# Gated attention and a token-mixing MLP on one core: fp32 loads of v and z with casts on ScalarE and GpSimd, and one more turned block of scores

## The chip, the cores and the metric

The kernel runs on one core of a Trainium2 chip. The metric is device time in microseconds (us) of one execution: the median of a few runs, with the profile of one execution beside it. Engines are named as in the profile: PE is TensorE (PEld its weight loads), DVE is VectorE, ACT is ScalarE, POOL is GpSimd, SP is SyncE, which here only issues DMAs.

## The reference

Inputs: u and v of 8 x 3200 x 256, z of 8 x 3200 x 64, and three weights, all fp32.

```
scores = (z @ z.T) / S                    # per batch, 3200 x 3200
attn   = relu(scores) ** 2
x      = u * (attn @ v)                   # 3200 x 256
W_tok  = einsum('bsd,btd->bst', x @ w_q, x @ w_k) / sqrt(64)
out    = relu(einsum('bst,btd->bsd', W_tok, x)) @ w_out
```

The second half has no nonlinearity between W_tok and x, so the kernel forms `(x @ w_k).T @ x` ("heads", 64 x 256) first and then multiplies `x @ w_q` by it.

## The kernel before, in words

**Tiles.** The 3200 rows of a batch are 25 row tiles of 128, in seven groups: six of 512 columns (4 row tiles) and one of 128. A tile of scores is one group's columns against one row tile. Two tiles make a pair. For a pair, `scores` (L258) puts two fp16 matmuls with 64 contraction rows side by side into a PSUM tile of two banks (two such tiles exist, shared with the later products); `first_stage` (L278) takes max(0, x) times a constant to `g` in SBUF, on ACT (L286) or DVE (L290); `second_stage` (L296) squares `g` to fp16 `at`, on ACT (L306) or POOL (L308). `at` has 16 buffers, `g` 7.

**Turned blocks.** Scores are symmetric, so the block of group gi against the rows of group gj is the transpose of the block the other way round. `is_turned` (L213) says which blocks are taken so: gj up to two groups beyond gi (`FAR`), or gj the last group; `SKIP` and `EXTRA` (L210) are exceptions. For such a block `at` is turned by DMA transposes on SP's queue (L330) into `tt` (seven homes; `ttl` for the last group), and when group gj comes, `second_product` (L345) takes its weights from there, without a score matmul of its own.

**Second product.** For each group and each of its two halves, 25 row tiles are multiplied with v and accumulated in PSUM (L351; four banks, two per half). `gate` (L361) copies the sums out (L368), adds the two halves of the contraction (L369) and multiplies by u on POOL (L388). Then x is turned by a DMA (L400), projected by w_q and w_k (L417), the keys turned (L436) and multiplied with x (heads, L455), and once a batch is done, mixed (L483), passed through relu (L505 to L511), projected by w_out (L521), scaled (L546 on DVE, L551 on ACT) and stored (L552).

**The order of the work.** All of it is written out by a planner that runs while the kernel is built. It keeps a clock for each engine (L586 to L592) and for SP's queue and the DMA engines (`move` and `send`, L616 to L627): a `move` has a time from which it may go, a due time, an issue time, a time on the DMA engines, what to do when it has landed (`LANDS` later), and a condition. `flush` sends the ripe move that is due first. `squares` (L695) and `choose` (L660) pick the engine of a square and of a first stage by the clocks. The main loop (L1029) takes, in turn, something of the later products, a pair, or a step of the second product; `lead` bounds how far pairs run ahead of the steps. The constants (`SPARE`, `BIAS`, `LATE`, `RING`, `UNTIL`, `XWAIT`) are weights of these choices, so altering one changes the order on every engine.

**v and z.** Batch 0 has its own loads (`load_first_z`, `load_first_v`). For batches 1 to 7, `batch_begun` (L843) has z loaded in one DMA (L156) and v in five of 5 row tiles (L150). These are issued by POOL and cast from fp32 to fp16 on the way. z is then turned by four DMA transposes on SP's queue (L163) to `zT`.

Of the kernel before, what the change touches and what calls it, by code (L numbers as in the profile page):

```python
# [10 lines left out]
FP32 = mybir.dt.float32  # L11
# [5 lines left out]
def kernel(  # L17
# [45 lines left out]
    pk = ctx.enter_context(tc.tile_pool(name="pk", bufs=3))  # L63
    pxt = ctx.enter_context(tc.tile_pool(name="pxt", bufs=NXT))
    pu = ctx.enter_context(tc.tile_pool(name="pu", bufs=2))
    pg = ctx.enter_context(tc.tile_pool(name="pg", bufs=7))
    psum = ctx.enter_context(tc.tile_pool(name="psum", bufs=3))
    pat = ctx.enter_context(tc.tile_pool(name="pat", bufs=NAT))
    ptt = ctx.enter_context(tc.tile_pool(name="ptt", bufs=1))
# [74 lines left out]
            nc.tensor.matmul(out=idle[:, 0:P], lhsT=blank, rhs=blank, start=True, stop=True)  # L144
        clock[PE] += 0.053 * cold() * n

    def load_v(b, n0, nn):
        if n0 == 0:
            vs[b] = pv.tile([P, NT, D], FP16, tag="v_sb", name="v_sb")
        nc.gpsimd.dma_start(out=vs[b][:, n0 : n0 + nn, :], in_=rows(v, b)[:, n0 : n0 + nn, :])  # L150

    ztimes = []
    ZTURNS = [(0, 0, 7), (1, 0, 7), (0, 7, 13), (1, 7, 13)]

    def load_z(b):
        nc.gpsimd.dma_start(out=zn[:, 1 : NT + 1, :], in_=rows(z, b))  # L156

    def turn_z(b, i):
        odd, m0, m1 = ZTURNS[i]
# [452 lines left out]

    def at_time(t, fn):
# [41 lines left out]

    FARDUE = 12.0
    SPLIT = 0.2
    UNTIL = 24.0

    def choose(a, d):  # L660
        t = shut() + LATE
# [33 lines left out]
    def squares():  # L695
        while pending and pending[0][0] <= clock[PE] + 0.3:
            ready, p, g = pending.pop(0)
            a, c = max(clock[ACT], ready), max(clock[POOL], ready)
            by_act = a + SPARE < c and (a + 1.06 <= shut() + LATE or a + 2.5 < c)
            ways = [by_act]  # L700
            if clock[PE] < UNTIL and max(a + 0.63, c + 1.05) + SPLIT < min(a + 1.06, c + 1.9):
                ways = [a < c, a >= c]
                done = max(give(ACT, ready, 0.63), give(POOL, ready, 1.05))
            else:
                done = give(ACT, ready, 1.06) if by_act else give(POOL, ready, 1.9)
            for (b, gi, gj, _, nn, _, _), turn in second_stage(p, g, ways):
# [3 lines left out]
                move(  # L710
                    done + SLACK, due + SLACK, 1.28, 0.21 * n, turn,
                    lambda t, x=(p, b, gi, gj, nn): block_landed(t, *x),
                    lambda x=(b, gi, gj): has_home(*x),
                )
            for x in tiles[2 * p : 2 * p + 2]:
                row_at[x] = done + 0.6
# [15 lines left out]
    def use_keys(b, gi):  # L732
        open_slot()
        ps = ps_tile("qk")
        prior = None
        if keyed and keys_at.get(keyed[0], 1e9) <= clock[PE]:
            prior = keyed.pop(0)
        projections(b, gi, ps, stop=not prior)
        clock[PE] += 0.44 if gi < LASTG else 0.24
        if prior:  # L740
            heads(*prior, ps, halves(gi))
            clock[PE] += 0.44 if prior[1] < LASTG else 0.11
        ready = clock[PE] + FROM_PE
        a, d = (max(clock[x], ready) for x in (ACT, DVE))
        by_act = a + 0.58 <= d + 0.69 or d + 0.69 > shut() + LATE + 0.6
        projections_out(b, gi, ps, by_act)
        done = give(ACT, ready, 0.58) if by_act else give(DVE, ready, 0.69)
        n = widths[gi] / P
        final = (b, gi) == (last, LASTG - 2)
        if not final:  # L750
            move(
                done + SLACK, done + 10.0, 1.28, 0.21 * n, lambda: turn_keys(b, gi),
                lambda t: at_time(t, lambda: double(b, gi)),
            )
            keyed.append((b, gi))
        if prior:
            heads_out(*prior, ps)
            done = give(DVE, done, 0.7)
            if prior[1] == LASTG:
                give(POOL, done, 0.6)  # L760
                heads_known(prior[0])
        close_slot(done)
        if len(keyed) == 2 and gi == LASTG:
            add_extra(done + 14.0, "heads", use_heads)
        if final:
            for _ in keyed[1:]:
                add_extra(done, "heads", use_heads)
# [49 lines left out]
    def project_out(b, gi, ps, ready):  # L817
# [11 lines left out]
            if gi < LASTG:  # L829
                stored[i] = t  # L830

        move(done + SLACK, done + 6.0, 0.55, 1.6, stores[0], landed)

    def push(takes):
        give(POOL, clock[PE], 0.6)
        dma_at[0] = max(dma_at[0], clock[PE]) + takes

    Z0 = 24
    ZWAIT, ZDUE, ZSTEP, ZSTEP0 = 14.0, 32.0, 7.0, 5.0
    V0 = 56  # L840
    V1 = 10

    def batch_begun(b, t):  # L843
        if b + 1 < B:
            t0 = max(t + 6, Z0)
            at_time(t0, lambda: (load_z(b + 1), push(3.0)))
            step = ZSTEP if b else ZSTEP0
            for i, (_, m0, m1) in enumerate(ZTURNS):
                move(
                    t0 + ZWAIT + step * i, t0 + ZDUE + step * i, 1.28, 0.21 * (m1 - m0),  # L850
                    lambda i=i: turn_z(b + 1, i),
                    lambda t, i=i: z_ready.update({(b + 1, i): t}),
                )
            for i in range(5):
                at = t + 20 + 13 * i if b else V0 + V1 * i
                at_time(at, lambda i=i: v_loaded(b + 1, 5 * i, 5))

    def v_loaded(b, n0, nn):
        load_v(b, n0, nn)
        push(2.5)  # L860
        for n in range(n0, n0 + nn):
            v_at[b, n] = dma_at[0] + 5.0

    z_ready = {}

# [4 lines left out]
    def group_begun(b, gi, t):  # L870
        if gi == 0:
            batch_begun(b, t)
        if gi + 1 < NG:
            move(max(t + 2, clock[POOL] + SLACK), t + 7, 0.55, 1.6, lambda: load_u(b, gi + 1))
        elif b + 1 < B:
            move(max(t + 2, clock[POOL] + SLACK), t + 7, 0.55, 1.6, lambda: load_u(b + 1, 0))

    SPARE = 0.5
    BIAS = 0.2
    XDUE = 5.0  # L880
    XWAIT = 2.0
    LATE = 0.5

    def half_done(b, gi, half):
        ready = clock[PE] + FROM_PE
# [9 lines left out]
        if half == halves(gi)[-1]:  # L895
            n = 8 if widths[gi] == W else 2
            move(
                t + SLACK, t + XDUE, 1.28, 0.21 * n, lambda: turn_x(b, gi),
                lambda t: x_landed(t, b, gi), lambda: len(xTs) < NXT,
            )  # L900

# [119 lines left out]
    move(10.0, 14.0, 0.55, 1.6, lambda: load_u(0, 0))  # L1021
# [153 lines left out]
```

## Time and profile before

| | |
|---|---|
| median of 3 runs | 774.47 us (774.18 to 778.38) |
| the profiled execution | 773.15 us |
| its span from first to last instruction | 770.9 us |
| mean granted TensorE clock in it | 0.997 |
| instructions | 28221 |
| bytes read from HBM, written to it | 59.64 MB, 26.21 MB |

The profile's page gives each engine's busy time and its share of the span, forty slices of the span in tenths, the DMA queues, the chain of waits that ended last, and the costliest groups of instructions by line with their mean duration in ns and the idle time of their engine before them. A busy TensorE is modelled: its matmuls are pipelined, so the chain is read beside it. Further views used below: busy time by stretch (length, then busy time and count of PE, PEld, DVE, ACT and POOL, granted clock, DMA share, GB/s), groups by line and shape, waits (who waited for whom: us in total, times, longest), one tile's instructions, and the chain in order of time (start, length, what).

### The profile page before, as it was taken

To read this page: it belongs to the slowest core of one execution; us is meant where nothing else is said; L and a number is where in the kernel's file an instruction comes from. 1 tells how busy PE (TensorE), PEld (TensorE's weight loads), DVE (VectorE), ACT (ScalarE), POOL (GpSimd) and SP (SyncE) were. 2 spreads that over 40 slices of the span, in tenths; PEclk is the share of its full clock that TensorE was granted. 3 is DMA by queue.
4 is the path that set the end of the run, shared out by engine and by line. 5 is a ranking of instruction groups with operands and counts; after the bars stand their busy time and mean duration, and the time that the engine had idled before them with its cause. 6 is when DMAs were issued, how large, how long until landed. Compare 5 with 4: busy or idle time off the path is not lost.

```text
span 770.9 us, 28221 instructions
## 1 busy us (share of the span) xinstructions
PE 761.7 (99%) x12408; PEld 678.4 (88%) x12408; DVE 510.5 (66%) x537; ACT 561.2 (73%) x647; POOL 591.1 (77%) x496
## 2 busy tenths in 40 slices
PE   8999999999999999999999999999999999999996
PEld 7889998888898888989889988998889989898884
DVE  6775876675787566765677756765667476675645
ACT  7785876778758678875788677877777676777734
POOL 8796788789687778666778687887878887888740
PEclk9999999999999999999999999999999999999998
DMA  8999999999999999999899999999999998979625
GB/s 199 130 187 182 167 204 173 160 212 194 194 162 189 194 209 190 182 213 203 153 190 162 188 231 163 219 145 160 262 156 192 184 190 211 201 143 203 152 84 191
DMA packets 307114, 141.09 MB, mean 183 GB/s; under 512 B 285744, under 2 KB 288432, under 8 KB 306992
## 3 DMA queue, kind: packets, MB, share of 16 engines
q1 hardware_dynamic: 300224, 123.13, 85.0%
q0 software_dynamic: 6624, 15.98, 14.8%
q8 instruction: 97, 1.59, 0.9%
q14 instruction: 25, 0.20, 0.1%
q10 hardware_dynamic: 144, 0.20, 0.1%
HBM read 59.64 MB, written 26.21 MB: 111 GB/s over the span
## 4 chain that ended last, share of the span: by engine, by line
PE 94%; POOL 2%; DVE 1%; DMA 1%; ACT 1%; issue 1%; POOLq 0%; SPq 0%; DVEq 0%; ACTq 0%
PE acc L351 68%; PE sc L263 13%; PE fo L521 6%; PE qk L417 3%; PE qk L455 2%; POOL at L308 2%; PE mx L483 1%; DMA z<-in_z_dram 1%; POOL x_sb L388 1%; DVE g L290 0%; ACT g L286 0%; DVE fo L546 0%; DMA xT_sb<-x_sb 0%; PE hd L455 0%; ACT at L306 0%
## 5 line engine op out<-in xcount | busy, mean ns | idle before, releaser
L351 PE MATMUL acc<-v_sb,at 64*128 64x256 f16 x7344 | 504.7, 269 | 0.0
L308 POOL TENSOR_TENSOR at<-g 128x1024 f16<-128x1024 f32 (+1 forms) x218 | 402.3, 1859 | 71.6 <-ACT g L286 29.1
L351 PEld LDWEIGHTS <-at 64*128 64x128 f16 x7344 | 407.2, 94 | 48.1 <-issue 4.8
L290 DVE TENSOR_SCALAR g<-sc 128x1024 f32<-128x1024 f32 (+2 forms) x285 | 338.5, 1203 | 122.8 <-PE sc L263 114.3
L306 ACT ACTIVATE at<-g 128x1024 f16<-128x1024 f32 (+2 forms) x255 | 257.2, 1023 | 21.8 <-DVE g L290 17.8
L286 ACT ACTIVATE g<-sc 128x1024 f32<-128x1024 f32 (+2 forms) x186 | 183.2, 989 | 76.8 <-PE sc L263 75.0
L388 POOL TENSOR_TENSOR x_sb<-both,u_sb 128x512 f16<-128x512 f32 (+1 forms) x112 | 135.8, 1217 | 81.6 <-DVE both L369 77.7
L263 PE MATMUL sc<-zT 64*128 64x512 f16 x924 | 188.1, 375 | 1.4 <-DVE g L290 0.6
L351 PE MATMUL acc<-v_sb,tt 64*128 64x256 f16 x2272 | 163.4, 269 | 0.0
L351 PEld LDWEIGHTS <-tt 64*128 64x128 f16 x2272 | 126.2, 94 | 10.3
L369 DVE TENSOR_TENSOR both<-acc,both 128x512 f32<-128x512 f32 (+1 forms) x104 | 69.6, 670 | 21.4 <-ACT both L368 17.0
L263 PEld LDWEIGHTS <-zT 64*128 64x128 f16 x924 | 61.2, 94 | 7.6 <-issue 3.9
L368 ACT COPY both<-acc 128x512 f32<-128x512 f32 (+1 forms) x69 | 39.0, 565 | 38.7 <-PE acc L351 36.1
L546 DVE TENSOR_SCALAR fo<-fo 128x1024 f32<-128x1024 f32 (+1 forms) x28 | 32.4, 1166 | 46.6 <-PE fo L521 46.6
L509 ACT ACTIVATE rt<-mx 128x1024 f16<-128x1024 f32 x39 | 39.9, 1024 | 12.6 <-PE mx L483 12.1
L521 PE MATMUL fo<-wo,rt 128*128 128x256 f16 x386 | 46.6, 273 | 0.5 <-ACT rt L505 0.5
L521 PEld LDWEIGHTS <-rt 128*128 128x128 f16 x386 | 36.2, 98 | 8.4 <-issue 3.6
L431 ACT CAST qk<-qk 128x512 f16<-128x512 f32 (+1 forms) x47 | 25.3, 539 | 24.6 <-PE qk L455 20.0
L368 DVE COPY both<-acc 128x512 f32<-128x512 f32 (+1 forms) x35 | 23.6, 674 | 21.2 <-PE acc L351 19.9
L470 DVE TENSOR_TENSOR ha<-qk,ha 128x512 f32<-128x512 f32 x37 | 25.5, 689 | 14.4 <-ACT qk L431 14.1
L551 ACT ACTIVATE fo<-fo 128x1024 f32<-128x1024 f32 (+2 forms) x23 | 22.5, 978 | 16.5 <-PE fo L521 15.8
L417 PE MATMUL qk<-xT_sb,wqk 64*128 64x256 f16 (+1 forms) x404 | 32.3, 265 | 0.0
(55 smaller groups left out, 282.9 us busy)
## 6 DMA issues: line engine op xcount, KB each, us to landing
u_sb<-in_u_dram SPq DMA_DIRECT2D x48, 512.0 KB, 4.8
out_dram<-fo SPq DMA_DIRECT2D x46, 512.0 KB, 5.1
v_sb<-in_v_dram POOLq DMA_DIRECT2D x35, 320.0 KB, 6.0
zn<-in_z_dram POOLq DMA_DIRECT2D x7, 400.0 KB, 7.8
tt<-at SPq DMA_TRANSPOSE x143, 4.7
u_sb<-in_u_dram SPq DMA_DIRECT2D x8, 128.0 KB, 2.9
out_dram<-fo SPq DMA_DIRECT2D x4, 256.0 KB, 3.3
xT_sb<-x_sb SPq DMA_TRANSPOSE x56, 5.4
```

What stands on the lines that cost most here:

```text
L263: nc.tensor.matmul(out=sc[h][:, 0:gw] if banks else sc[:, h, 0:gw], lhsT=z_cols(b, h, ti * P, P), rhs=z_cols(b, h, gs, gw), start=True, st ...
L286: nc.scalar.activation(out=g[:, hs, 0:w], in_=part, func=RELU, scale=GSCALE)
L290: nc.vector.tensor_scalar(out=g[:, hs, 0:w], in0=part, scalar1=0.0, scalar2=GSCALE, op0=AOP.max, op1=AOP.mult,)
L306: nc.scalar.square(out=out, in_=g[:, hs, 0:w])
L308: nc.gpsimd.tensor_mul(out=out, in0=g[:, hs, 0:w], in1=g[:, hs, 0:w])
L351: nc.tensor.matmul(out=accs[half, r][:, ds((j % 2) * D, D)], lhsT=weights(b, gi, ti, j)[top(r), :], rhs=vs[b][top(r), ti, :], start=(first ...
L368: copy(out=both[:, 0 : n * D], in_=accs[half, 0][:, 0 : n * D])
L369: nc.vector.tensor_add(out=both[:, 0 : n * D], in0=accs[half, 1][:, 0 : n * D], in1=both[:, 0 : n * D])
L388: nc.gpsimd.tensor_mul(out=xs[b, gi][:, 0:n, :, r, :].rearrange("p n c d -> p (n c) d"), in0=both[:, 0 : n * D].rearrange("p (m d) -> p m ...
L417: nc.tensor.matmul(out=ps[:, r, 0 : n * P], lhsT=wqk[top(r), c, :, :].rearrange("p t h -> p (t h)"), rhs=xTs[b, gi][top(r), 0:n, c, :], st ...
L509: nc.scalar.activation(out=out, in_=part, func=RELU)
L521: nc.tensor.matmul(out=banks[r][:, ds(j * D, D)], lhsT=flat[:, ds((dc * n + j) * P, P)], rhs=wo[:, dc, :], start=(dc == 0 and j == 0), sto ...
```

## The change

1. **Loads.** v and z of batches 1 to 7 are no longer cast in flight. They come as fp32 pieces on SP's queue into two staging tiles that alternate (3 and 2 row tiles of v, or 12 and 8 of z: 384 or 256 KB; the last piece of a z is 5 row tiles), one buffer each. When a piece has landed by the plan, ScalarE or GpSimd casts it to `v_sb` or `zn`. A piece is sent only when the plan has its staging tile free, and pieces go in a fixed order: per batch z in 3, then v in 10.
2. **One more turned block.** `EXTRA = [(0, 3)]`: in batches 1 to 7 the block of the first and the fourth group is turned too.
3. **Buffers.** `g` has 6 buffers in place of 7, and the staging tiles take 5 KB a partition.
4. **The planner's numbers.** A transpose of n blocks is planned as 0.2 + 0.13 n us of the DMA engines (0.21 n before); loads and stores 1.7 (1.6). `send` counts the DMA time from the end of the issue. `RING`, `SPARE`, `BIAS`, `XWAIT`, `LATE`, `UNTIL`, `lead` and the times of z's and v's loads are altered, and the third-issued load of v in batch 0 (row tiles 4 to 11) is planned at 6.2 instead of 9.0. `zn`'s border is cleared a second time, on GpSimd.

```diff
-    pg = ctx.enter_context(tc.tile_pool(name="pg", bufs=7))
+    pst = ctx.enter_context(tc.tile_pool(name="pst", bufs=1))
+    pg = ctx.enter_context(tc.tile_pool(name="pg", bufs=6))
...
-    def load_v(b, n0, nn):
-        if n0 == 0:
+    STAGES = (3, 2)
+    stage_of, parts = {}, []
+    turn = 0
+    for b in range(1, B):
+        for what, size in ((z, dqk), (v, D)):
+            n0 = 0
+            while n0 < NT:
+                nn = min(STAGES[turn] * D // size, NT - n0)
+                parts.append((b, what is v, n0, nn, turn))
+                n0, turn = n0 + nn, 1 - turn
+
+    def load_part(b, is_v, n0, nn, k):
+        if is_v and n0 == 0:
             vs[b] = pv.tile([P, NT, D], FP16, tag="v_sb", name="v_sb")
-        nc.gpsimd.dma_start(out=vs[b][:, n0 : n0 + nn, :], in_=rows(v, b)[:, n0 : n0 + nn, :])
+        stage = pst.tile([P, STAGES[k] * D], FP32, tag=f"st{k}", name="st")
+        size, what = (D, v) if is_v else (dqk, z)
+        stage_of[k] = stage[:, 0 : nn * size].rearrange("p (n d) -> p n d", d=size)
+        nc.sync.dma_start(out=stage_of[k], in_=rows(what, b)[:, n0 : n0 + nn, :])
+
+    def cast_part(b, is_v, n0, nn, k, by_act):
+        copy = nc.scalar.copy if by_act else nc.gpsimd.tensor_copy
+        out = vs[b][:, n0 : n0 + nn, :] if is_v else zn[:, 1 + n0 : 1 + n0 + nn, :]
+        copy(out=out, in_=stage_of[k])
...
-    EXTRA = []
+    EXTRA = [(0, 3)]
...
-    V3 = 9.0
+    V3 = 6.2
...
-    RING = 2.0
+    RING = 1.5
...
-        dma_at[0] = max(dma_at[0], begun) + takes
         sp_at[0] = max(begun + issue, dma_at[0] - RING)
+        dma_at[0] = max(dma_at[0], begun + max(issue, 0.9)) + takes
         if landed:
-            landed(max(sp_at[0], dma_at[0]) + LANDS)
+            landed(dma_at[0] + LANDS)
...
-    UNTIL = 24.0
+    UNTIL = 16.0
...
+            for i, x in enumerate(mine):
+                at = t0 + Z1 * i if not is_v else t + V2 + V3 * i if b else V0 + V1 * i
+                move(
+                    at, at + 8.0, 0.45, 0.2 + 1.5 * x[3] * (D if is_v else dqk) / 1024,
+                    lambda x=x: part_sent(*x),
+                    lambda t, x=x: at_time(t, lambda: part_landed(*x)),
+                    lambda x=x: parts[0] == x and stage_free[x[4]] <= clock[PE],
+                )
...
+    def part_landed(b, is_v, n0, nn, k):
+        n = nn * (D if is_v else dqk)
+        a, c = (max(clock[x], clock[PE]) for x in (ACT, POOL))
+        t_act, t_pool = 0.19 + 0.00084 * n, 0.15 + 0.0009 * n
+        by_act = a + SPARE < c and (a + t_act <= shut() + LATE or a + 2.5 < c)
+        cast_part(b, is_v, n0, nn, k, by_act)
...
-    SPARE = 0.5
-    BIAS = 0.2
+    SPARE = 0.1
+    BIAS = 0.0
     XDUE = 5.0
-    XWAIT = 2.0
-    LATE = 0.5
+    XWAIT = 7.0
+    LATE = 0.3
...
-    lead = 140
+    lead = 160
```

More of the change, by code (lines that the diff above doesn't have):

```diff
@@ L830, in landed @@
                 stored[i] = t
[L832 to L836, printed above, removed]
+        move(done + SLACK, done + 6.0, 0.45, 1.7, stores[0], landed)
     Z0 = 24
-    ZWAIT, ZDUE, ZSTEP, ZSTEP0 = 14.0, 32.0, 7.0, 5.0
-    V0 = 56
-    V1 = 10
-    def batch_begun(b, t):
[L844 to L847, printed above, removed]
+    Z1 = 3.0
@@ new lines, in part_sent @@
+    def part_sent(*x):
+        assert parts.pop(0) == x
+        stage_free[x[4]] = 1e9
+        load_part(*x)
+    def part_landed(b, is_v, n0, nn, k):
[4 more added lines that the diff above has]
+        cast_part(b, is_v, n0, nn, k, by_act)
+        done = give(ACT, clock[PE], t_act) if by_act else give(POOL, clock[PE], t_pool)
+        stage_free[k] = done + SLACK
+        if is_v:
+            v_at.update({(b, n): done + 0.3 for n in range(n0, n0 + nn)})
+        elif n0 + nn == NT:
+            step = ZSTEP if b > 1 else ZSTEP0
@@ L848, in batch_begun @@
             for i, (_, m0, m1) in enumerate(ZTURNS):
                 move(
-                    t0 + ZWAIT + step * i, t0 + ZDUE + step * i, 1.28, 0.21 * (m1 - m0),
-                    lambda i=i: turn_z(b + 1, i),
-                    lambda t, i=i: z_ready.update({(b + 1, i): t}),
-                )
[L854 to L862, printed above, removed]
+                    done + ZWAIT + step * i, done + ZDUE + step * i, 1.25, 0.2 + 0.13 * (m1 - m0),
```

29 lines of the change are left out of this document (21 added, 8 removed).

## The prediction

> **What bounds the kernel now.** I read the page first (busy shares, slices, chain), then the busy time by stretch, then what TensorE waits for.
>
> ```profile
> PE 761.7 (99%) x12408; PEld 678.4 (88%) x12408; DVE 510.5 (66%) x537; ACT 561.2 (73%) x647; POOL 591.1 (77%) x496
> PEclk9999999999999999999999999999999999999998
> PE 94%; POOL 2%; DVE 1%; DMA 1%; ACT 1%; issue 1%; POOLq 0%; SPq 0%; DVEq 0%; ACTq 0%
> PE acc L351 68%; PE sc L263 13%; PE fo L521 6%; PE qk L417 3%; PE qk L455 2%; POOL at L308 2%; PE mx L483 1%; DMA z<-in_z_dram 1%; POOL x_sb L388 1%; DVE g L290 0%; ACT g L286 0%; DVE fo L546 0%; DMA xT_sb<-x_sb 0%; PE hd L455 0%; ACT at L306 0%
> ```
>
> ```profile
> 0.00:20.00 20.00, 18.05 (x232) 14.52 (x234) 13.46 (x17) 14.29 (x18) 16.59 (x21) 1.00 0.80 194
> 20.00:110.00 90.00, 89.26 (x1491) 82.53 (x1489) 65.66 (x69) 68.17 (x77) 71.27 (x61) 1.00 1.12 175
> 200.00:290.00 90.00, 90.00 (x1490) 79.24 (x1486) 62.83 (x66) 61.84 (x71) 68.41 (x60) 1.00 1.12 192
> 470.00:560.00 90.00, 89.89 (x1476) 80.57 (x1474) 56.02 (x59) 70.58 (x79) 74.42 (x62) 1.00 1.09 191
> 740.00:771.00 31.00, 24.54 (x332) 18.91 (x328) 15.17 (x21) 9.84 (x21) 5.18 (x4) 0.93 0.45 162
> ```
>
> ```profile
> PE sc L263 <- DVE g L290: 0.6, 2, 0.4
> ```
>
> In a row by stretch the first number after the length is TensorE's busy time. From 200 to 290 us it is 90.00 of 90; from 20 to 110 it lacks 0.74 us, from 470 to 560 it lacks 0.11 us; only the first 20 us (1.95 us) and the last 31 us (6.46 us) have real holes. The score matmuls' largest wait sums to 0.6 us in the whole run. The chain of waits agrees: 94% of it is TensorE, at a granted clock of nine tenths or more, and the rest is mostly the start and the end. So time is won by fewer TensorE instructions and lost by any new hole in that row; work that only moves between the other engines is free as long as they keep up.
>
> Two prices of TensorE come from a stretch of the chain in which nothing else stands:
>
> ```profile
> 27.85 0.22 PE sc L263 x2
> 28.07 0.98 PE acc L351 x18
> ```
>
> A pair of score matmuls (x2) moves the chain on by 0.22 us, an accumulating matmul by 0.98 / 18 = 0.054 us. The whole chain says the same: 13% of 770.9 us over 462 pairs is 0.217 us each.
>
> The Trainium skill ("Perfetto Trace Analysis", section "Identifying the Most-Contended Engine") calls matmul busy time a poor measure of how near TensorE is to its limit and asks for weight-load busy time beside it. By that rule PEld at 88% would leave an eighth of slack, and taking matmuls out might bring nothing; that each pair moves the chain speaks against it. It stands among the rivals.
>
> **The change part by part.** Counts are from the order of instructions of the two kernels, engine by engine.
>
> *The turned block.* The scores of group 0's rows against group 3 are computed once in each of batches 1 to 7 and used again in group 3 through a DMA transpose: 4 x 4 tiles a batch, of which 4 score matmuls of 512 columns fall away, 28 in all (916 to 888), or 14 pairs. The accumulating matmuls stay 10000 (7344 to 7120 from `at`, 2272 to 2496 from `tt`). TensorE: 14 x 0.22 = **3.1 us less**. What is late next: nothing, since TensorE is followed by TensorE there. With each pair one first stage and one square go, and 14 transposes of 8 blocks come (141 to 155).
>
> *Loads and casts.* 42 casting DMAs on GpSimd's queue (35 of v, 7 of z) become 13 fp32 pieces a batch (10 of v, 3 of z) on SP's queue, 91 in all, and 91 casts. ScalarE gets 29 of 768 elements a partition, 24 of 512, 6 of 320; GpSimd 13, 18 and 1.
>
> ```profile
> L308 POOL TENSOR_TENSOR at<-g 128x1024 f16<-128x1024 f32 x211 | 396.5, 1893 | 70.0 <-ACT g L286 29.1 <-DVE g L290 29.0 <-issue 9.6
> L290 DVE TENSOR_SCALAR g<-sc 128x1024 f32<-128x1024 f32 x278 | 335.2, 1221 | 121.8 <-PE sc L263 113.3 <-POOL at L308 3.3 <-ACT g L286 1.8
> L306 ACT ACTIVATE at<-g 128x1024 f16<-128x1024 f32 x240 | 250.8, 1056 | 21.8 <-DVE g L290 17.8
> L286 ACT ACTIVATE g<-sc 128x1024 f32<-128x1024 f32 x175 | 178.8, 1023 | 75.0 <-PE sc L263 73.2 <-POOL kx L448 0.9 <-POOL hs L477 0.6
> L368 ACT COPY both<-acc 128x512 f32<-128x512 f32 x63 | 36.8, 584 | 34.3 <-PE acc L351 31.7 <-PE sc L263 1.1 <-PE hd L455 1.0
> L546 DVE TENSOR_SCALAR fo<-fo 128x1024 f32<-128x1024 f32 x25 | 30.4, 1224 | 44.1 <-PE fo L521 44.0
> L368 DVE COPY both<-acc 128x512 f32<-128x512 f32 x33 | 22.8, 689 | 19.5 <-PE acc L351 18.3 <-PE sc L263 0.5 <-POOL x_sb L388 0.2
> L551 ACT ACTIVATE fo<-fo 128x1024 f32<-128x1024 f32 x21 | 21.5, 1024 | 15.6 <-PE fo L521 14.8 <-DMA u_sb<-in_u_dram 0.8
> L150 POOL DMA_DIRECT2D v_sb<-in_v_dram x35 | 20.7, 591 | 0.0
> L124 ACT CAST zd<-z 128x512 f16<-128x512 f32 x1 | 0.6, 619 | 1.8 <-DMA z<-in_z_dram 1.8
> L124 POOL CAST zd<-z 128x512 f16<-128x512 f32 x1 | 0.6, 609 | 0.9 <-DMA z<-in_z_dram 0.9
> L124 ACT CAST zd<-z 128x384 f16<-128x384 f32 x1 | 0.5, 507 | 0.0
> L124 POOL CAST zd<-z 128x384 f16<-128x384 f32 x1 | 0.5, 503 | 1.4 <-DMA z<-in_z_dram 1.4
> ```
>
> A cast of 512 elements takes ScalarE 0.62 us and one of 384 takes 0.51; the line through both gives 0.84 us for 768 and 0.45 for 320. GpSimd: 0.61, 0.50, so 0.82 and 0.45.
> - ScalarE: 29 x 0.84 + 24 x 0.62 + 6 x 0.45 = 42.0 us of casts. The plan takes 16 squares (16.9 us), 10 first stages (10.2) and 13 copies of sums (7.6) from it and gives it 16 outputs (16.4). Net 42.0 - 16.9 - 10.2 - 7.6 + 16.4 = +23.7: 585 us, 76% of the span.
> - GpSimd: 13 x 0.82 + 18 x 0.61 + 0.45 = 22.1 us of casts, less 42 DMA issues x 0.591 = 24.8, plus a square (1.9): about -0.8.
> - VectorE: 4 first stages and 16 outputs fewer, 13 copies more: -4.9 - 19.6 + 9.0 = -15.5.
>
> No engine comes near its span, so this costs nothing; the cover is the room that these engines have, 186 us on ScalarE afterwards. If the cover were gone altogether it would be the 42.0 us of ScalarE's casts.
>
> *The new wait.* A cast waits on ScalarE or GpSimd for its piece. Queued behind it on ScalarE are first stages, squares and copies of sums; a held first stage holds one of the two score tiles, and TensorE's next score matmul waits for that. No such wait stands in the trace; the nearest are loads of u on the same queue:
>
> ```profile
> u_sb<-in_u_dram SPq DMA_DIRECT2D x48, 512.0 KB, 4.8
> v_sb<-in_v_dram POOLq DMA_DIRECT2D x35, 320.0 KB, 6.0
> tt<-at SPq DMA_TRANSPOSE x143, 4.7
> u_sb<-in_u_dram SPq DMA_DIRECT2D x8, 128.0 KB, 2.9
> ...
> q1 hardware_dynamic: 300224, 123.13, 85.0%
> q0 software_dynamic: 6624, 15.98, 14.8%
> ```
>
> ```profile
> L174 SPq DMA_DIRECT2D u_sb<-in_u_dram x56: 327/529/1814, 5.0 to 738.3; - x56
> ...
> DMA to landing us min/median/max: 2.0/4.7/7.6
> ```
>
> A piece has 384 KB or less (3 x 256 fp32 on 128 partitions). Between 2.9 us for 128 KB and 4.8 for 512 KB that is about 4.2 us, an estimate (the casting loads of v, which move 640 KB of fp32, took 6.0); the kernel's plan allows 0.9 + 0.2 + 1.125 + 4.0 = 6.2 us plus what is queued, so the median piece is 2 us early. The longest landing of u, 7.6, is 1.4 us past the plan. Cost: from nothing to 59 casts on ScalarE x 1.4 = 83 us; I take **nothing**, nearest the median row, and keep a part of the upper end for the range.
>
> *SP's queue.* 105 more instructions (452 to 557): 91 x 0.529 = 48.1 us, and 14 transposes.
>
> ```profile
> L330 SPq DMA_TRANSPOSE tt<-at x143: 1231/1354/5576, 17.1 to 713.4; - x143
> ```
>
> ```profile
> SPq L330 <- POOL at L308: 51.2, 37, 2.8
> SPq L330 <- ACT at L306: 48.7, 32, 5.4
> SPq L330 <- ACT g L286: 42.7, 17, 9.9
> ```
>
> 14 x 1.354 = 19.0 us: 67 us in all. SP stood waiting for work 142.6 us in these three rows alone, which hides it. Moved bytes: v and z were 14.8% x 770.9 = 114 us of the 16 DMA engines (batch 0's v included); now each of 7 batches moves 4000 KB, at (4.8 - 2.9) us for 384 KB at most 19.8 us, so up to 139 us, and 14 transposes of 256 KB come on top. The engines are as full as before or somewhat fuller. I take nothing: in the stretch from 200 to 290 us their share is 1.12 and TensorE misses nothing.
>
> The Trainium skill ("DMA: Bandwidth & Descriptors", section "Queues, rings and completion order") speaks against this step: each DMA engine serves one queue's descriptors in ring order and takes turns between queues. By it the old loads shared the engines with the transposes, and the new ones stand in front of them; no run here shows yet what that costs.
>
> *Start and end.* Batch 0's own score matmuls are not reduced, but its pairs are dealt out differently (squares split between two engines until 16 instead of 24, a load of v on GpSimd moved ahead of a half square with a clearing of `zn`).
>
> ```profile
> 7.40 2.04 POOL at L308 x2
> ...
> 10.00 10.30 POOL at L308 x6
> ```
>
> The chain passes through GpSimd's squares here, so a load ahead of one can cost its issue, 0.59 us and some tenths, about 0.8; a better split can win at most the holes of the first two stretches, 1.95 + 0.74 = 2.7 us, of which the first stretch, with the landing of z in it, keeps a part whatever is done. I take 0, between +0.8 and -2.7. The order at the end is the same: 0.
>
> **Sum.** The profiled execution took 773.15 us (span 770.9 and 2.25 around it). 773.15 - 3.1 = 770.1. The median of the runs shown, 774.47, lies 1.3 above that execution, so the forecast is 774.47 - 3.1 = **771.4 us**, 0.4% faster. A difference of 0.5% (3.9 us) is about what a measurement of this kernel can tell from none: under 770.6 counts as faster, over 778.3 as slower.
>
> **The rivals.**
> 1. *More than the matmuls.* The new dealing-out also removes the holes of the first 110 us and the 0.11 later: 3.1 + 1 to 2.8, so 768.6 to 770.4. For it: the chain's start is squares on GpSimd, which ScalarE and GpSimd now split differently. Against: the holes are small.
> 2. *Late casts (slower).* Place: ScalarE, batches 1 to 7. Price 1.4 us a late cast. It decides from 7.0 us on (the 3.1 gained and 3.9 more): five of 59 casts reaching TensorE in full. Eight of them: 771.4 + 11.2 = 782.6; three: 775.6, within the bound. For it: landings up to 7.6 us, SP's queue fuller, two stages only. Against: 2 us of room at the median.
> 3. *Transposes behind the pieces.* In one queue each piece holds the transposes behind it by up to 1.9 us; 91 x 1.9 = 173 us of delay, of which 4% on TensorE already undoes the gain. If 2% does: 771.4 + 3.5 = 774.9. For it: the ring order; against: transposes land in 4.7 us today beside the same bytes.
> 4. *The removed pairs bring nothing.* If TensorE's row hides slack, the run stays at 774.5.
>
> **How the numbers follow.** Forecast 0.50, of which a third falls under 770.6 by the spread of the start (0.17 faster, 0.33 same); rival 1: 0.25 (faster); rival 2: 0.12 (0.09 slower, 0.03 same); rival 3: 0.08 (0.03 slower, 0.05 same); rival 4: 0.05 (same). Faster 0.42, same 0.46, slower 0.12. The range goes from 768.5 (3.1 + 2.8 below 774.47) to 777.0, which takes in rivals 3 and 4 and the mild end of rival 2; about 0.1 lies above it.
>
> **What would show it.** Right: 896 score matmuls at 0.22 us a pair, TensorE's row still full from 110 us on, a span near 767.8; casts with almost no idle time before them put down to the DMA. Wrong: ScalarE or GpSimd idle for tens of us before casts and score matmuls waiting for `g` or `at` (rival 2); accumulating matmuls that wait for `tt`, transposes landing well over 4.7 us (rival 3); holes in the first 110 us that grow; or 14 fewer pairs at an unchanged span (rival 4).

## The result and the profile after

The changed kernel takes 800.12 us (median of 6 runs, 797.72 to 807.63), beside 776.14 us of the kernel before on the same chip (6 runs). The ratio is 1.032, with a 95% interval of 1.026 to 1.038: 3.2% slower, some 24 us, where 0.4% faster was forecast. Here and below a ratio leaves out executions more than 1.5% above the fastest of their kernel. The profiled execution took 797.92 us, its span is 796.1 us.

The page of the changed kernel: busy times, chain and DMA queues.

```profile
PE 763.3 (96%) x12380; PEld 679.8 (85%) x12380; DVE 506.9 (64%) x544; ACT 569.1 (71%) x670; POOL 592.7 (74%) x489
...
q1 hardware_dynamic: 328112, 155.48, 99.2%
q0 software_dynamic: 576, 1.64, 1.0%
...
PE 82%; DMA 8%; ACT 5%; SPq 2%; issue 1%; DVE 1%; POOL 1%; POOLq 0%; ACTq 0%; DVEq 0%
PE acc L368 59%; PE sc L280 12%; DMA st<-in_v_dram 6%; PE fo L538 5%; PE qk L434 3%; PE qk L472 2%; ACT g L303 1%; ACT at L323 1%; PE mx L500 1%; POOL x_sb L405 1%; ACT rt L526 1%; DMA z<-in_z_dram 1%; DMA out_dram<-fo 1%; SPq L347 1%; ACT v_sb L170 0%
```

The engines' busy times hardly moved, and no engine is fuller than before. What moved is the time in which TensorE is not busy: 770.9 - 761.7 = 9.2 us before, 796.1 - 763.3 = 32.8 us now, and the difference is about the time lost. The chain moved with it: TensorE falls from 94% to 82% of it, and the landing of v's pieces, which was not there, has 6%. The busy time by stretch (TensorE's is the first number after the length) shows where. Two stretches of the kernel before:

```profile
110.00:200.00 90.00, 90.00 (x1486) 78.18 (x1483) 57.88 (x63) 67.34 (x75) 75.81 (x63) 1.00 1.01 182
290.00:380.00 90.00, 90.00 (x1500) 82.49 (x1496) 62.42 (x66) 67.69 (x78) 66.57 (x57) 1.00 1.03 183
```

And of the changed kernel:

```profile
20.00:110.00 90.00, 85.24 (x1428) 80.02 (x1425) 62.79 (x64) 67.11 (x79) 75.32 (x58) 1.00 1.02 187
110.00:200.00 90.00, 84.97 (x1385) 77.97 (x1382) 57.89 (x63) 63.61 (x74) 65.89 (x55) 0.98 1.09 205
200.00:290.00 90.00, 90.00 (x1468) 79.56 (x1465) 56.46 (x61) 68.92 (x80) 67.27 (x59) 1.00 1.11 218
290.00:380.00 90.00, 85.41 (x1401) 76.35 (x1399) 53.60 (x58) 64.42 (x76) 64.47 (x54) 0.98 1.05 205
```

Before, TensorE lacked 0.74 us from 20 to 110 us and nothing in the other three stretches; now three of the four lack 4.6 to 5.0 us each. Who waited for whom in the changed kernel (us in total, times, longest):

```profile
ACT v_sb L170 <- DMA st<-in_v_dram: 46.0, 22, 5.0
...
POOL v_sb L170 <- DMA st<-in_v_dram: 19.5, 10, 5.4
...
POOL kx L465 <- DMA kx<-qk: 15.9, 11, 3.3
```

ScalarE and GpSimd stand 65.5 us at casts of v. The landings are not long in themselves. The last number of a DMA row is its median from issue to landing:

```profile
st<-in_v_dram SPq DMA_DIRECT2D x35, 384.0 KB, 4.5
...
tt<-at SPq DMA_TRANSPOSE x157, 4.4
```

A piece of 384 KB lands after 4.5 us, within the plan's 6.2, and the turns of `at` after 4.4 us, not longer than before. It is the issue that comes late. One of the long waits, from the timeline of the changed kernel (start, length, engine, instruction, and in brackets the idle time before it):

```profile
349.70 1.24 SPq L417 DMA_TRANSPOSE xT_sb<-x_sb  x1
...
351.04 2.22 SPq L347 DMA_TRANSPOSE tt<-at  x1
...
352.64 0.59 ACT L385 COPY both<-acc 128x512 f32<-128x512 f32 x1 [0.68 <-PE acc L368]
...
353.35 0.53 SPq L165 DMA_DIRECT2D st<-in_v_dram  x1
...
358.17 0.83 ACT L170 CAST v_sb<-st 128x768 f16<-128x768 f32 x1 [4.95 <-DMA st<-in_v_dram]
358.58 1.01 SPq L165 DMA_DIRECT2D st<-in_v_dram  x1
358.91 1.02 ACT L526 ACTIVATE rt<-mx 128x1024 f16<-128x1024 f32 x1
```

ScalarE is through with everything ahead of the cast at 353.23, 0.12 us before SP even issues the piece; the cast begins 4.8 us after that issue, and the relu (L526) of a later product stands queued behind it. The other waits are alike: pairing pieces and casts of this trace in their order, 28 casts waited over 1 us, and at the median their engine was free 2.2 us after the piece's issue, where the plan allows 6.2.

### The profile page after: what moved, and what is told of

It is laid out like the page before. It is cut to its first block, busy times and chain, and to the rows that moved or that the text cites. A ratio compares the mean times of both kernels' runs of the same rounds, so it can differ in the third digit from the quotient of the medians.

```text
span 796.1 us, 28355 instructions
## 1 busy us (share of the span) xinstructions
PE 763.3 (96%) x12380; PEld 679.8 (85%) x12380; DVE 506.9 (64%) x544; ACT 569.1 (71%) x670; POOL 592.7 (74%) x489
## 4 chain that ended last, share of the span: by engine, by line
PE 82%; DMA 8%; ACT 5%; SPq 2%; issue 1%; DVE 1%; POOL 1%; POOLq 0%; ACTq 0%; DVEq 0%
PE acc L368 59%; PE sc L280 12%; DMA st<-in_v_dram 6%; PE fo L538 5%; PE qk L434 3%; PE qk L472 2%; ACT g L303 1%; ACT at L323 1%; PE mx L500 1%; POOL x_sb L405 1%; ACT rt L526 1%; DMA z<-in_z_dram 1%; DMA out_dram<-fo 1%; SPq L347 1%; ACT v_sb L170 0%
## 5 line engine op out<-in xcount | busy, mean ns | idle before, releaser
L368 PE MATMUL acc<-v_sb,at 64*128 64x256 f16 x7120 | 493.3, 270 | 1.1 <-ACT both L385 0.6
L325 POOL TENSOR_TENSOR at<-g 128x1024 f16<-128x1024 f32 (+2 forms) x220 | 406.4, 1858 | 88.0 <-DVE g L307 73.8
L307 DVE TENSOR_SCALAR g<-sc 128x1024 f32<-128x1024 f32 (+1 forms) x285 | 337.3, 1193 | 153.4 <-PE sc L280 148.1
L323 ACT ACTIVATE at<-g 128x1024 f16<-128x1024 f32 (+1 forms) x240 | 240.0, 1018 | 23.8 <-DVE g L307 21.0
L303 ACT ACTIVATE g<-sc 128x1024 f32<-128x1024 f32 (+2 forms) x172 | 170.9, 999 | 49.2 <-PE sc L280 43.5
L368 PE MATMUL acc<-v_sb,tt 64*128 64x256 f16 x2496 | 177.5, 270 | 0.0
L368 PEld LDWEIGHTS <-tt 64*128 64x128 f16 x2496 | 139.7, 94 | 12.9 <-DMA xT_sb<-x_sb 0.2
L170 ACT CAST v_sb<-st 128x768 f16<-128x768 f32 (+1 forms) x43 | 31.8, 739 | 46.1 <-DMA st<-in_v_dram 46.0
L568 ACT ACTIVATE fo<-fo 128x1024 f32<-128x1024 f32 (+2 forms) x39 | 37.3, 993 | 15.8 <-PE fo L538 14.9
L526 ACT ACTIVATE rt<-mx 128x1024 f16<-128x1024 f32 x36 | 36.8, 1022 | 9.8 <-PE mx L500 9.8
L465 POOL COPY kx<-kx 128x128 f16<-128x128 f16 (+1 forms) x99 | 25.9, 292 | 15.9 <-DMA kx<-qk 15.9
```

The lines of the kernel that those rows point to most:

```text
L303: nc.scalar.activation(out=g[:, hs, 0:w], in_=part, func=RELU, scale=GSCALE)
L307: nc.vector.tensor_scalar(out=g[:, hs, 0:w], in0=part, scalar1=0.0, scalar2=GSCALE, op0=AOP.max, op1=AOP.mult,)
L323: nc.scalar.square(out=out, in_=g[:, hs, 0:w])
L325: nc.gpsimd.tensor_mul(out=out, in0=g[:, hs, 0:w], in1=g[:, hs, 0:w])
L368: nc.tensor.matmul(out=accs[half, r][:, ds((j % 2) * D, D)], lhsT=weights(b, gi, ti, j)[top(r), :], rhs=vs[b][top(r), ti, :], start=(first ...
L526: nc.scalar.activation(out=out, in_=part, func=RELU)
```

## The experiments

The theory after the result, A: the pieces come later than the plan's casts, and that wait is the loss. Rivals: B, the pieces hold the transposes behind them in SP's queue; C, the turned block or the planner's numbers make a worse order. As runs came in, D (the new numbers of the queue are too short), E and F (the queue has no room for the block's transposes), G (any new order costs this) and H (only the planner's answer to the block) were set against each other. Ratios are to the kernel before, run on the same chip, with 95% intervals.

**e1: the casting loads back, block and numbers kept.**

```diff
-        nc.sync.dma_start(out=stage_of[k], in_=rows(what, b)[:, n0 : n0 + nn, :])
+        nc.gpsimd.dma_start(out=vs[b][:, n0 : n0 + nn, :], in_=rows(v, b)[:, n0 : n0 + nn, :])
...
```

> The casting loads of GpSimd come back as before (5 of v, 1 of z a batch); the turned block and all the planner's new numbers stay. Theory A (the pieces arrive later than the plan has their casts, and ScalarE and GpSimd stand still for 66 us at them): no casts, so the loss goes, 771 to 776 us. Theory B (the pieces stand before the transposes in SP's queue and hold them): the same, 771 to 778. Theory C (the turned block or the new numbers make a worse order): stays at 793 to 800.

Measured: 1.012 (1.007 to 1.017), 779 to 800 us from run to run. Between the theories: most of the loss goes with the pieces and casts, but not all of it.

**e2: no turned block, pieces and numbers kept.**

```diff
-    EXTRA = [(0, 3)]
+    EXTRA = []
```

> The fp32 pieces and casts and the new numbers stay; the turned block of groups 0 and 3 is left out (14 more score pairs, 3.1 us of TensorE). Theory A: the casts still wait for tens of us, 795 to 803 us. Theory B: 141 instead of 155 turns in SP's queue, some relief, 785 to 795. Theory C with the block as the cause: 774 to 778.

Measured: 790.25 us, 1.019 (1.015 to 1.022). This is in theory B's range. The block is a part of the loss, the larger part stays.

**e3: casts planned 4 us later.**

```diff
-                    lambda t, x=x: at_time(t, lambda: part_landed(*x)),
+                    lambda t, x=x: at_time(t + 4.0, lambda: part_landed(*x)),
```

> Each cast is planned 4 us later than the plan has its piece landed; the rest as changed (the order on all engines is planned anew, staging tiles come free later). Theory A: most idle time before casts goes (66 us to under 20), 775 to 785 us. Theory B: the pieces go the same way through the queue, 793 to 800, with the idle time elsewhere. Theory C: 793 to 800.

Measured: 795.78 us, 1.025 (1.022 to 1.029). The casts' own waiting went, as theory A had it, and most of the time lost did not come back. Its waits show other places:

```profile
POOL kx L465 <- DMA kx<-qk: 31.2, 14, 5.8
POOL v_sb L170 <- DMA st<-in_v_dram: 8.4, 4, 7.4
ACT v_sb L170 <- DMA st<-in_v_dram: 3.2, 3, 1.5
```

```profile
PE acc L368 <- POOL v_sb L170: 8.6, 2, 7.6
```

11.6 us before casts instead of 65.5, but now the second product once stands 7.6 us for a row of v, and GpSimd's wait for the turned keys `kx` has doubled, from 15.9 to 31.2 us. Later casts and staging tiles that come free later mostly moved the wait.

**e4: the casts wait for no load.** They read a small fixed tile; the order and the DMAs are those of the changed kernel, except that a piece no longer waits for the cast that read its staging tile before (in the changed kernel SP waits 4.8 us for casts of v with its pieces).

```diff
-        copy(out=out, in_=stage_of[k])
+        copy(out=out, in_=still[:].unsqueeze(1).broadcast_to(out.shape))
```

> The order of the changed kernel, with every piece still loaded, but the casts read a small fixed tile in place of the piece, so that they wait for no load; v and z of batches 1 to 7 are therefore not the inputs. Theory A: the wait is all of the loss: 770 to 777 us, with TensorE's row full again. Theory B: the transposes are still late: 790 to 800, waits on tt, xT and kx. Theory C: 793 to 800.

Measured: 1.007 (1.004 to 1.011), against 1.032 with the wait. So by the ratios about three quarters of the loss reaches TensorE through this wait; the executions scatter, 778 to 792 us. That is the way the loss takes; it does not yet say why the pieces are late. And the pieces are not the only late landings. In the profiled execution, at 791.65 us the longest of the ten, GpSimd stands far longer at the keys than in the changed kernel (15.9 us):

```profile
POOL kx L469 <- DMA kx<-qk: 78.9, 19, 9.7
```

**e5: the block alone on the kernel before.**

```diff
-    EXTRA = []
+    EXTRA = [(0, 3)]
```

> The kernel before with only the block of groups 0 and 3 turned in batches 1 to 7. Theory D (the new numbers by which the planner reckons SP's queue and the DMA engines are too short, so that every consumer of a DMA stands too early in the order; neither the block nor the pieces are the root): TensorE saves 3.1 us and nothing waits, 772 to 776 us. Theory E (14 more transposes in a queue that is already full are the root): 783 to 790 us, waits on kx, xT and tt.

Measured: 793.92 us, 1.023 (1.017 to 1.030): the block costs 18 us without pieces, casts or new numbers, where 3.1 us of TensorE should have been won. Theory D alone falls. The time is above theory E's range too, and E's sign, long waits for landings, is nearly absent. Who waited for score tiles (0.6 us before) and for keys in it, and a piece of its chain:

```profile
PE sc L263 <- DVE g L290: 7.9, 15, 1.1
...
POOL kx L448 <- DMA kx<-qk: 1.0, 2, 0.5
```

```profile
284.19 0.22 PE sc L263 x2
284.41 0.11 PE acc L351 x2
284.52 0.23 PE sc L263 x2
...
284.84 1.03 ACT g L286
...
286.86 1.01 ACT g L286
...
287.91 0.39 PE sc L263 x2
```

From 284.75 to 287.91 the chain is ScalarE's first stages and a square, not TensorE, and score pairs stand close together. A likely reading, which no view of the plan shows: by the old, longer numbers the planner sees the turned rows land late, has no row left to multiply, and lays score pairs next to each other.

**e8: the new numbers of the queue alone on the kernel before.**

```diff
-    RING = 2.0
+    RING = 1.5
-        dma_at[0] = max(dma_at[0], begun) + takes
         sp_at[0] = max(begun + issue, dma_at[0] - RING)
+        dma_at[0] = max(dma_at[0], begun + max(issue, 0.9)) + takes
-                    done + SLACK, due + SLACK, 1.28, 0.21 * n, turn,
+                    done + SLACK, due + SLACK, 1.25, 0.2 + 0.13 * n, turn,
...
```

> The kernel before with only the planner's numbers of SP's queue and the DMA engines changed (0.2 + 0.13 n in place of 0.21 n for a transpose, 1.7 for 1.6, RING 1.5, the order of the two clocks in send). Same instructions but for their order. Theory D: 783 to 792 us, GpSimd waiting for kx by tens of us. Theory E: 774 to 778, no such wait.

Measured: 789.54 us, 1.019 (1.014 to 1.025), as theory D had it. The same instructions, only their order differs, and consumers stand before their landings. The wait for keys in the kernel before, and two waits in e8:

```profile
POOL kx L448 <- DMA kx<-qk: 2.2, 2, 2.0
```

```profile
POOL kx L448 <- DMA kx<-qk: 26.1, 13, 3.7
...
PE qk L417 <- DMA xT_sb<-x_sb: 3.8, 1, 3.8
```

The packets in the trace of the kernel before show what the two numbers are. A turned block is 128 packets of 256 bytes (e14b's 112 blocks add 14336 of them), and 16 engines share them. Their mean is 26.7 ns, 0.213 us a block: the old 0.21. Their median is 18 ns, 0.144 us a block, near the new 0.13. The mean is higher because one packet in a hundred takes over 100 ns. The new number, 1.24 us for 8 blocks against 1.71 by the mean, leaves these stalls out.

**e7: the changed kernel with the old numbers of the queue.** The edit is e8's the other way.

> The changed kernel with the old numbers of SP's queue and the DMA engines, everything else as changed (pieces, casts, block, SPARE, BIAS, LATE, XWAIT, UNTIL, lead). Theory D: the casts stand later in the order and wait under 20 us in all, 773 to 782 us. Theory E: 790 to 800.

Measured: 789.56 us, 1.016 (1.012 to 1.020): half the loss is back, not all, so neither D nor E alone. The casts hardly wait now, and TensorE waits for score tiles instead:

```profile
POOL v_sb L170 <- DMA st<-in_v_dram: 5.8, 4, 2.4
...
ACT v_sb L170 <- DMA st<-in_v_dram: 2.3, 2, 1.4
```

```profile
PE sc L280 <- DVE g L307: 9.3, 14, 1.2
```

**e9: e7 without the block**, so the pieces and casts alone, with the change's other numbers.

> As the run with the old queue numbers, and without the turned block: the pieces and casts alone, on the old reckoning of the queue. Theory D: 775 to 782 us, about 3 us above that run's TensorE time. Theory E: 774 to 778 here, and 10 us or more below the run with the block.

Measured: 776.68 us, 1.000 (0.997 to 1.002). This fits both theories' ranges. The 91 pieces and casts, and the sixth buffer of `g` in place of seven, cost nothing that can be measured when the queue is reckoned as before:

```profile
ACT v_sb L170 <- DMA st<-in_v_dram: 5.7, 1, 5.7
...
POOL v_sb L170 <- DMA st<-in_v_dram: 1.7, 4, 0.6
```

**e13: the change's other numbers alone on the kernel before** (SPARE, BIAS, LATE, XWAIT, UNTIL, lead, V3).

> The kernel before with only the change's other numbers (SPARE 0.1, BIAS 0, LATE 0.3, XWAIT 7, UNTIL 16, lead 160, V3 6.2): no pieces, no block, the old reckoning of the queue. Theory F: an order planned anew, with the same instructions and transposes, 773 to 778 us. Theory G: 783 to 795.

Measured: 776.87 us, 1.001 (0.998 to 1.003). So an order planned anew need not cost anything, and theory G falls.

The runs so far, as ratios to the kernel before. All but the first, e5 and e8 also have the change's other numbers, which cost nothing by themselves (e13):

| | no block | block turned |
|---|---|---|
| casting loads, old queue numbers | 1 | 1.023 (e5) |
| casting loads, new queue numbers | 1.019 (e8) | 1.012 (e1) |
| pieces, old queue numbers | 1.000 (e9) | 1.016 (e7) |
| pieces, new queue numbers | 1.019 (e2) | 1.032 (the change) |

In three rows the block costs 1.3 to 2.3%. In the second it does not: 1.019 (1.014 to 1.025) without it and 1.012 (1.007 to 1.017) with it. The two causes do not simply add up.

**e10: the block left out of the scores, but not turned.** Its weights come from a fixed tile.

```diff
-            if is_turned(b, gi, gj):
+            if is_turned(b, gi, gj) and not (b and (gi, gj) in EXTRA):
...
+        if b and (gj, gi) in EXTRA:
+            return still[:]
```

> The kernel before with the scores of the block of groups 0 and 3 left out in batches 1 to 7 as in the run with the block alone, but the block is not turned: group 3 takes its weights for it from a fixed tile, so this part of the output is not the reference's. TensorE's work is that of the block alone, SP's queue that of before. Theory F (14 more transposes are what the queue cannot take): 770 to 775 us. Theory G (any order planned anew, or the missing pairs, costs the 18 us): 785 to 795.

Measured: 774.1 us, 0.999 (0.996 to 1.002), against 1.023 with the transposes. So the removal of the pairs harms nothing, and the transposes of the block are what costs (theory F), be it by their load or by the plan's waiting for their landing, which is gone here too. The 3.1 us, 0.4%, lie just inside this interval; they were neither seen nor excluded.

**e11 and e12: the block alone, between the two reckonings.**

```diff
-                    done + SLACK, due + SLACK, 1.28, 0.21 * n, turn,
+                    done + SLACK, due + SLACK, 1.28, 0.19 * n, turn,
```

> The block alone on the kernel before, with 0.19 n in place of 0.21 n for a transpose's time on the DMA engines. Theory F: the order no longer holds TensorE back for score tiles, but the landings come later than planned and are waited for: 778 to 790 us. Theory G: 785 to 795. If there is room for the block between the two reckonings: 770 to 775.

> The block alone on the kernel before, with 0.16 n for a transpose and every landing reckoned 2 us later (LANDS 6). Theory F: 775 to 785 us, less waiting for landings than on the changed kernel. Theory G: 785 to 795. Room for the block: 770 to 775.

Measured: 784.76 us, 1.007 (1.002 to 1.011), and 785.38 us, 1.011 (1.005 to 1.016). Better than e5's 1.023, and still no win. Score tiles are hardly waited for now (0.9 us in e11); landings are again. From e11:

```profile
POOL kx L448 <- DMA kx<-qk: 20.4, 8, 6.8
```

**e14, e15, e16: spare DMAs on the kernel before**, its order on the four other engines unchanged: 28 transposes of 4 blocks, the 112 blocks of the turned block, into a tile that nobody reads; or 28 copies of 16 KB, or of 128 KB.

```diff
+                if x[0] and x[1] == 0 and group_of(x[2]) == 3:
+                    at, at0 = made[x]
+                    at_time(done + SLACK, lambda a=at[:, at0 : at0 + W]: more(a))
...
+    def more(a):
+        nc.sync.dma_start_transpose(out=spare[:], in_=a)
```

> The kernel before, its order on TensorE, VectorE, ScalarE and GpSimd unchanged, with the 112 blocks of the extra turned block turned besides (28 transposes of 4 blocks, planned by nobody, into a spare tile that nobody reads). Theory F (the queue has no room for them): whatever is queued behind them lands late, 782 to 795 us. Theory H (the queue has room; it is the planner that answers the block with a worse order): 774 to 778.

> The same with 28 copies of 16 KB (128 bytes a partition) in place of the transposes: SP's issue time alone, 28 x 0.5 us, and almost no time on the DMA engines. If SP's issue is what is short: a third to a half of the loss of the spare transposes. If the DMA engines or the turning are short: 774 to 778 us.

> The same with 28 copies of 128 KB, the bytes of the transposes without the turning. If bytes on the DMA engines are short: near the spare transposes, 780 to 795 us. If it is the turning (many packets of 256 bytes, and the change between copies and transposes): 774 to 780 us.

Measured: 1.047 (1.041 to 1.053), 1.020 (1.014 to 1.026) and 1.031 (1.026 to 1.036). The first (810.24 us) and the third (797.85 us) lie above all the ranges, and the second (789.87 us) would fit SP's issue as what is short. But these three measure something else besides. All 28 write one spare tile, and SP waits for the landing of the one before. What SP's queue waited for in e14 and in e15:

```profile
SPq L723 <- DMA spare<-at: 34.9, 16, 5.1
```

```profile
SPq L723 <- DMA spare<-at: 41.0, 16, 6.4
```

What they show, beside e15b below, is that SP's queue cannot be held: 41 us of SP waiting in all, with next to no bytes, cost 15 us of time.

**e14b and e15b: the same with four spare tiles in turn**, so that none waits for the one before (`g` with 6 buffers, to make room).

> The 28 spare transposes of 4 blocks again, on the order of before, into four spare tiles in turn (and g with 6 buffers, as in the changed kernel, to make room), so that none waits for the landing of the one before it, which in the first such run held SP's queue. Theory F (the queue has no room): 785 to 805 us, a part of the first run's loss. If the first run's loss was that wait alone: 774 to 778 us.

> The 28 copies of 16 KB again, with four spare tiles in turn. SP's issue time alone: 28 x 0.48 = 13 us put into the queue where a batch begins. Theory F by issue time: 782 to 790 us. If the first run's loss was the wait for the landing before: 774 to 778 us.

Measured: 1.012 (1.008 to 1.016) with the transposes, 1.000 (0.998 to 1.003) with the small copies. Of each, the spare DMAs' issue time in ns (least, median, most), GpSimd's wait for keys, and the share that the two DMA queues read; the transposes first, then the copies:

```profile
L725 SPq DMA_TRANSPOSE spare<-at x28: 1189/1257/2201, 101.7 to 672.0; - x28
...
POOL kx L449 <- DMA kx<-qk: 23.9, 11, 6.0
...
q1 hardware_dynamic: 315456, 126.80, 86.9%
q0 software_dynamic: 6624, 15.98, 16.2%
```

```profile
L725 SPq DMA_DIRECT2D spare<-at x28: 465/566/689, 104.0 to 668.8; - x28
...
POOL kx L449 <- DMA kx<-qk: 12.0, 5, 4.7
...
q1 hardware_dynamic: 304256, 123.59, 86.2%
q0 software_dynamic: 6624, 15.98, 16.0%
```

28 issues, about 16 us of SP's time, go in for nothing. 28 transposes, which nobody waits for, cost some 10 us, and what is waited for longer are other DMAs, the keys: theory H falls, and F holds in part. The sum of a wait is not its price, though: e15b's 12.0 us at the keys cost nothing. The 10 us are half of what the block costs in e5. That the planner's answer to it, or the wait for its landings, is the other half is an inference from two different orders.

Two things are not separated here. The transposes hold SP longer, 28 x 1.257 = 35 us against 16. And they move 128 KB each against 16 KB: the run that would tell turning from bytes, copies of 128 KB with four spare tiles, is missing. With one spare tile the big copies cost more than the small ones (e16 and e15, 1.031 and 1.020, with intervals that touch), which speaks for bytes; that the pieces raise the bytes of the two queues from 139.11 to 153.44 MB for nothing (e9) speaks against them.

**e18: the changed kernel with the loads of u on GpSimd's queue.**

```diff
-        nc.sync.dma_start(out=us[b, gi][:, 0:nn, :], in_=rows(u, b)[:, n0 : n0 + nn, :])
+        nc.gpsimd.dma_start(out=us[b, gi][:, 0:nn, :], in_=rows(u, b)[:, n0 : n0 + nn, :])
+        give(POOL, clock[PE], 0.6)
```

> The changed kernel with the 56 loads of u issued by GpSimd, planned there at 0.6 us each and still reckoned on SP's queue too (so that the plan is the more careful by about 0.5 us a load); 56 x 0.53 = 30 us leave SP's queue. Theory F (SP's queue runs behind the plan): most of the loss goes, 775 to 788 us, and casts wait under 25 us. If the DMA engines themselves are short (the bytes are the same): 790 to 800 us.

Measured: 802.41 us, 1.032 (1.026 to 1.038), a little above both ranges, and the casts wait as before:

```profile
ACT v_sb L170 <- DMA st<-in_v_dram: 39.6, 18, 5.4
POOL v_sb L170 <- DMA st<-in_v_dram: 27.9, 9, 6.4
```

56 issues fewer in SP's queue help nothing, though the order is another one too. With e15b this speaks against SP's issue time as what is short, and for the DMA engines; neither run excludes a part of the former. No version among these beats the kernel before.

## Why the prediction was wrong, point by point

- **What bounds the kernel: right, and not the whole.** TensorE was full, and the holes that opened in its row, 32.8 us in place of 9.2, are about the time lost. But a full row is kept full by DMAs that land when the order expects them, and the views that were read do not show how much room these have. That it was small is what e5, e8 and e14b show, each by itself.
- **"14 x 0.22 = 3.1 us less. What is late next: nothing": this failed.** The pairs did go (896 score matmuls), and a pair still costs 0.22 us in the changed kernel's chain:

```profile
346.55 0.22 PE sc L280 x2
346.77 0.76 PE acc L368 x14
```

  But TensorE's busy time did not fall with them (763.3 us, 761.7 before; 760.1 in e10), and no run shows the 3.1 us as time. What is late next are the turned rows and what goes through the DMA engines with them. Without the transposes the block is harmless (e10); with them it costs 2.3% (e5).
- **"SP stood waiting for work 142.6 us ..., which hides it. I take nothing": the step that failed first.** The sum asked for room in SP's time, and 28 more issues were indeed free (e15b). The 14 transposes were put at nothing on the DMA engines too, and there they are not free: e14b's 112 more blocks cost 1.2%. By the mean of the kernel before, 0.213 us a block, 112 blocks are 24 us of all 16 engines, an estimate that the prediction did not make. The DMA share of 1.12 in a stretch without holes was read as room. The share does not tell: the two queues read 99.8% before, 103.1% in e14b, which loses 1.2%, and 102.2% in e15b, which loses nothing. Nor is all of the 142.6 us spare time beside the issues: such a wait can lie inside the duration of an issue (the longest of the row `tt<-at`, 5576 ns, holds a wait of 4.5 us for GpSimd), and a queue that waits holds what stands behind it (e15 beside e15b).
- **The planner's numbers were not priced.** The working looked at their effect on the first 20 us alone. The shorter reckoning of a transpose puts consumers ahead of their landings: 1.9% by itself (e8), and the same with the pieces (e2 beside e9).
- **"The new wait ... I take nothing", upper end 1.4 us a cast: mis-sized, and the place was right.** The 2 us of room were counted from a piece's issue. The landings kept to it (4.5 us at the median); the issues did not, they came late for the casts. The waits sum to 65.5 us, up to 5.4 us each, and carry about three quarters of the loss (e4). With the queue reckoned as before they shrink to 8.1 us (e7) and 7.4 us (e9).
- **Casts and loads as work: right.** Casts of 768 elements of v were put at 0.84 us on ScalarE and 0.82 on GpSimd and took 0.83 and 0.82; e9 puts pieces and casts together at nothing. The sums by engine were off without harm: ScalarE gained 7.9 us and not 23.7, VectorE lost 3.6 and not 15.5, in part because relus and casts of qk moved to VectorE, which the sums leave out. The ring order that the prediction takes from the Trainium skill ("DMA: Bandwidth & Descriptors", section "Queues, rings and completion order") was weighed as speaking against the pieces; with the queue reckoned as before it does not show in the time (e9, 1.000).
- **Rivals.** The second, late casts on ScalarE (and on GpSimd), is the way most of the loss took, with 0.12; the casts were late by their issues and not by long landings, and its time of 782.6 us was too low. The third named the turns' queue, but by a mechanism that is not seen: pieces alone hold nothing that costs time (e9). In its own sum 1.8% of 173 us, not 4%, already undoes the gain of 3.1. The first did not happen: TensorE's first 20 us are as before (17.85 us busy, 18.05 before), and the holes from 20 to 110 us grew from 0.7 to 4.8 us, which the prediction named as a sign of being wrong. The fourth, that the removed pairs bring nothing, stays open: e10's interval takes in both 3.1 us and nothing.

What stays open: how e4's last 0.7% and e1's 1.2% divide between the block's turning and the numbers, as runs of both scatter over 14 to 20 us; why the block costs less with pieces (e7, 1.6%) than without (e5, 2.3%), and nothing with the new numbers and casting loads (e1 beside e8); and whether it is the turning, the bytes or SP's longer issues by which the spare transposes cost what they do.

## What to carry to other kernels

Before trading matmuls for DMA transposes, ask whether the other DMAs can bear them. A full TensorE does not say so, and neither does the DMA share, which reads about 1 here in runs that lose time and in runs that do not. Spare transposes that nobody reads, put into the old order, do: they measure the load alone, if they do not wait for each other (e14b against e14). Where an order is fixed ahead of time, the reckoned duration of a DMA is a part of the design: with the block, the long number left holes (e5), and the short one put engines that work in order in front of landings (e8). Both cost about 2%. A wait is to be sized from when its DMA can be issued, not only from issue to landing; and an addition should be tried by itself first, since here the part that looked costly (91 more loads on SP's queue, 91 casts) was free and the part that looked free was not.

## What the runs showed of the hardware that had not been expected

- 28 transposes of four 128 x 128 fp16 blocks that nobody reads cost about 10 us (1.012) in a kernel whose two DMA queues read 99.8% of the engines' span; 28 copies of 16 KB at the same places cost nothing (1.000).
- In the kernel before, a packet of 256 bytes of a DMA transpose took 18 ns at the median and 26.7 on average, a packet of 4096 bytes 159 and 208 ns: by the medians 14 and 26 bytes a ns and engine. The transposes' 272512 packets fill 59% of the span of the 16 engines.
- With SP's queue held by waits for landings, 35 to 41 us in all, 28 spare DMAs cost 2.0% as copies of 16 KB and 4.7% as transposes (e15, e14); without these waits, nothing and 1.2% (e15b, e14b).
- Moving 56 loads of 512 KB or less from SP's queue to GpSimd's, on a kernel that loses its time to late landings, changed nothing (1.032 before and after).
